# An adaLN block with cached attention on one core: K and V loaded in pairs of tiles, all of K ahead of all of V

## The chip, the cores and the metric

The kernel runs on one NeuronCore of a Trainium2 chip. The core has a matrix engine (PE), a vector engine (DVE), a scalar engine (ACT), a general engine (POOL), a sequencer that here only issues transfers (SP), and 16 DMA engines that move bytes between the device memory (HBM) and the core's own memory. The metric is the device time of one execution in microseconds. Every transfer counts: inputs start in HBM and the output ends there.

## The reference

A transformer block for two sequences (B = 2), one new token each, model width D = 640, 32 heads of 192. Of the key and value caches only the last W = 1024 of 4096 positions are read. Cut to what matters:

```python
W = min(4096, max(256, Sk // 4))                       # 1024
q = (x @ wq).reshape(B, 1, 32, 192).transpose(0, 2, 1, 3)
k, v = k_cache[:, :, Sk - W:, :], v_cache[:, :, Sk - W:, :]
p = softmax(einsum('bhqd,bhkd->bhqk', q, k) * 192 ** -0.5)
a = einsum('bhqk,bhkd->bhqd', p, v).reshape(B, 1, 6144) @ wo

sa, ca, ga, sb, cb, gb = (silu(c) @ w_mod).reshape(B, 6, 1, 640)   # one each
h = layernorm(x) * (1 + ca) + sa
x = x + ga * attention(h)                              # the four lines above
h = layernorm(x) * (1 + cb) + sb
x = x + gb * ((gelu(h @ w_gate) * (h @ w_up)) @ w_down)
```

Everything is bf16 in HBM: `w_mod` 4.9 MB, `wq` and `wo` 7.9 MB each, the K and V parts 25.2 MB each, the three FFN weights 2.0 MB each. Each byte is read once.

## The kernel before, in words

**The layout of the attention.** The 128 partitions hold 32 heads times 4 groups of positions, so each partition owns 256 consecutive positions of one head for each sequence. A tile is 64 of them for all partitions: 64 * 192 values, 24576 bytes in a row, 3.1 MB in all. One sequence (b) has four K tiles and four V tiles (t = 0 to 3).

**Scores** (`d_mul` L452, `p_reduce` L458, `d_rows` L472). For each half tile (hf) DVE multiplies K in place by the query, which `qbc` holds on every partition (L454). PE then adds up the products: 12 matmuls of 512 columns with the identity as the weights (L465), 16 of the 192 products at a time into one PSUM bank, and DVE sums the 16 that are left into 32 scores (L474). `filler` puts four matmuls that nobody reads (L444) ahead of each such group.

**Softmax** (`softmax` L478), once for each sequence: DVE, PE and ACT pass a maximum along, ACT takes the exponentials (L493).

**Values** (`d_mask` L501, `p_pv` L506). DVE spreads the 64 weights of each partition into `Em`, a matrix with one column for each head and position (L502, two buffers), and PE multiplies it with the V tile: 32 matmuls of 384 columns for each tile (L514). `normalize` (L523) and `p_sel` (L536) bring the result into the layout of `wo`.

**What sets the order.** A recording layer (`_Sched`) keeps one list of operations for each engine, in the order in which the code declares them, and derives each wait from the buffers that an operation reads and writes. `emit` (L83) writes the five lists out, inside an `nc.Block()` (L665) that gives each engine its own block of code, entered and left by a branch. All large loads are issued by SP, in the order of its list.

**The ring.** K and V go through five slots of one tile each (`ring`, NS = 5). The order is the four K tiles of b = 0; then V of b = 0 and K of b = 1 in turn; then V of b = 1 (`items`, L322). A slot is loaded again as soon as the last reader of its tile has been declared and has finished (`declare_ring` L332). Ahead of the ring come `w_mod` (into slots 2 and 3) and `wq` in two parts (into `r1`, 61440 bytes a partition); behind it `wo` in four parts (into `r1` again, L585), `w_gate`, `w_up` in two parts and `w_down` in three (into slots that are free by then, L589 to L601).

**The work beside it.** While K of b = 1 is scored, V of b = 0 is multiplied (the loop at L546); V of b = 1 comes alone (L562). Then `oc` and its transposes `oT` (L578), the `wo` product in four parts (L609), layer norm, the FFN (L628, L651) and the store of 2.5 KB. `warm` (L440) puts matmuls without a reader between these small stages too, for instance 14 behind the second `p_sel`, 15 behind the second part of `wo`, 13 beside the second layer norm, 7 behind the first part of `w_down`.

Of the kernel before, what the change touches and what calls it, by code (L numbers as in the profile page):

```python
# [103 lines left out]
def bass_adaLN_cond__sliding_block_cached__geglu_ffn__decode_kernel(  # L104
# [34 lines left out]
    NTL = KP // J  # L139
    JH = J // 2  # L140
    NQ = H * Dh
# [4 lines left out]
    NQC = RN // QC  # L146
    SCALE = float(Dh) ** -0.5
# [6 lines left out]
    NS = 5  # L154
    SL = J * Dh
    WQ_SPLIT = [3, 2]
    assert sum(WQ_SPLIT) == KT
    WO_SPLIT = [16, 16, 12, 4]
    OT_SPLIT = [16, 16, 16]
    assert sum(WO_SPLIT) == NT and sum(OT_SPLIT) == NT  # L160
    WU_SPLIT = [3, 2]
    assert sum(WU_SPLIT) == KT
    WD_SPLIT = [6, 4, 2]
    assert sum(WD_SPLIT) == FT
    ND = 4

    WO_WARM = [2, 15, 2, 10]
    WD_WARM = [7, 2, 0]

    es = ExitStack()  # L170
    with es:
# [6 lines left out]
        ring = sb("ring", [P, NS, J, Dh], BF16)  # L178
        ring_f = ring[:, :, :, :].rearrange("p s j d -> p (s j d)")
        def slot_f(slot, a, n):  # L180
            assert a + n <= SL
            return ring_f[:, slot * SL + a:slot * SL + a + n]


        assert KT * 6 * D <= 2 * SL and 2 * KT * F + FT * D <= 2 * SL
        wm_f = ring_f[:, 2 * SL:2 * SL + KT * 6 * D]
        wm_v = wm_f.rearrange("p (k n) -> p k n", k=KT)
        Qsel = slot_f(4, 0, 2 * HM * P).rearrange("p (b m n) -> p b m n", b=2, m=HM)
        qC = slot_f(4, 2 * HM * P, RN)
        wg_v = ring_f[:, SL:SL + KT * F].rearrange("p (k n) -> p k n", k=KT)  # L190
        wu_v = ring_f[:, SL + KT * F:SL + 2 * KT * F].rearrange("p (k n) -> p k n", k=KT)
        wd_v = ring_f[:, SL + 2 * KT * F:SL + 2 * KT * F + FT * D].rearrange("p (f n) -> p f n", f=FT)
        oc = slot_f(4, 0, RN)
        oT = slot_f(4, RN, NT * SQ).rearrange("p (t m) -> p t m", m=SQ)
        aC = slot_f(3, 0, FN)
        aT = slot_f(3, FN, FT * SQ).rearrange("p (f m) -> p f m", m=SQ)
# [3 lines left out]
        one = sb("one", [1, 1], F32)  # L200
# [20 lines left out]
        Sg = sb("Sg", [P, max(KP, FN)], F32)  # L221
        S_sb = Sg[:, 0:KP]
        gl = Sg[:, 0:FN]
        ones_f = Sg[:, 0:P]
        M1 = sb("M1", [P, 1], F32)
        gm = sb("gm", [1, H], F32)
        gx = sb("gx", [1, H, QP], F32)
        nb = sb("nb", [P, 1], F32)
        E_sb = sb("E_sb", [P, KP], BF16)
# [7 lines left out]
        BK_O = 3  # L237
# [13 lines left out]
        sem_wq = [S.sem("d_wq%d" % i) for i in range(len(WQ_SPLIT))]  # L251
        sem_wo = [S.sem("d_wo%d" % i) for i in range(len(WO_SPLIT))]
        sem_wg = S.sem("d_wg")
        sem_wu = [S.sem("d_wu%d" % i) for i in range(len(WU_SPLIT))]
        sem_wd = [S.sem("d_wd%d" % i) for i in range(len(WD_SPLIT))]
        sem_ring = [S.sem("d_ring%d" % i) for i in range(NS)]
# [9 lines left out]
        def dram_rows(v):  # L266
# [7 lines left out]
        S.op("pool", lambda e: e.memset(one[:, :], 1.0), writes=["one"], name="one")  # L274
        S.op("pool", lambda e: e.memset(ones_f, 1.0), writes=[("S", 0, 0), ("S", 0, 1), ("S", 1, 0), ("S", 1, 1)], name="ones_f")
        S.op("pool", lambda e: e.affine_select(out=ident_f[:, :], in_=ones_f, pattern=[[-1, P]],
                                                compare_op=ALU.is_equal, fill=0.0, base=0, channel_multiplier=1),
             reads=[("S", 0, 0), ("S", 0, 1), ("S", 1, 0), ("S", 1, 1)], writes=["ident_f"], name="ident_f")
# [3 lines left out]
        S.op("pool", lambda e: e.memset(Qsel, 0.0), writes=[("ring", 4, 0)], name="Qsel0")  # L282
# [18 lines left out]
        for b in range(2):  # L301
            for m in range(HM):
                S.op("dve", (lambda b, m: lambda e: e.tensor_copy(
                    out=Qsel[:, b, m, :].rearrange("p (a m t) -> p a m t", a=NJ, m=HM)[:, :, m, :],
                    in_=ident_f[:, BS * b:P:SQ].unsqueeze(2).broadcast_to([P, NJ, QP])))(b, m),
                    reads=["ident_f"], writes=[("ring", 4, 0)], name="Qsel%d%d" % (b, m))

        def half_key(slot, hf):
            return ("ring", slot, hf)

        def ring_keys(slot):
            return [half_key(slot, 0), half_key(slot, 1)]

        keep = {}
        S.dma("sp", k_dma(wm_f, w_mod.rearrange("(p k) n -> p (k n)", k=KT)), sem_wm, writes=ring_keys(2) + ring_keys(3), name="ld_wm")
        wq_src = A_wq.rearrange("(p k) n -> p k n", k=KT)
        wq_of = [(sum(WQ_SPLIT[:i]), sum(WQ_SPLIT[:i + 1])) for i in range(len(WQ_SPLIT))]
        keep["wq_dma"] = [S.dma("sp", k_dma(wq_v[:, ka:kb, :].rearrange("p k n -> p (k n)"), wq_src[:, ka:kb, :].rearrange("p k n -> p (k n)")),
                                sem_wq[i], writes=[("wq", i)], name="ld_wq%d" % i) for i, (ka, kb) in enumerate(wq_of)]


        items = [("k", 0, t) for t in range(NTL)]  # L322
        for t in range(NTL):
            items += [("v", 0, t), ("k", 1, t)]
        items += [("v", 1, t) for t in range(NTL)]
        place = {it: n for n, it in enumerate(items)}
        ring_state = {"next": 0, "done": set()}

        def slot_of(*it):
            return place[it] % NS  # L330

        def declare_ring(*consumed, upto=len(items)):  # L332
            ring_state["done"].update(place[it] for it in consumed)
            while ring_state["next"] < upto and (ring_state["next"] < NS or (ring_state["next"] - NS) in ring_state["done"]):
                n = ring_state["next"]
                kind, b, t = items[n]
                slot = n % NS
                cache = A_v_cache if kind == "v" else A_k_cache
                S.dma("sp", k_dma(ring[:, slot, :, :].rearrange("p j d -> p (j d)"),
                                  cache[b, :, K0:Sk, :].rearrange("h (q r) d -> h q r d", q=QP)[:, :, J * t:J * (t + 1), :].rearrange("h q r d -> h q (r d)")),  # L340
                      sem_ring[slot], writes=ring_keys(slot), name="ld_%s%d_%d" % (kind, b, t))
                ring_state["next"] += 1

        declare_ring(upto=2)


# [37 lines left out]
        def mod_part(part):  # L384
# [10 lines left out]
            S.op("pe", f, reads=["scT"] + ring_keys(2) + ring_keys(3), writes=[bank(bk)], name="mod%d" % part)  # L395
# [9 lines left out]
        declare_ring(upto=4)  # L405


        for i, (ka, kb) in enumerate(wq_of):
            def f(e, ka=ka, kb=kb):
                last = None  # L410
                for k in range(ka, kb):
                    for c in range(NQC):
                        for j in range(NJ):
                            last = e.matmul(ps[SQ * j:SQ * j + SQ, BK_H + c, 0:QC], lhsT=hT[:, k, :],  # L414
                                            rhs=wq_v[:, k, RN * j + QC * c:RN * j + QC * (c + 1)],
                                            start=(k == 0), stop=(k == KT - 1), tile_position=(0, SQ * j), skip_group_check=True)
                return last
            keep["q"] = S.op("pe", f, reads=["hT", ("wq", i)], writes=[bank(BK_H + c) for c in range(NQC)], name="q%d" % i)

# [5 lines left out]

        for c in range(NQC):
            move(("act", "dve")[c % 2], qC[:, QC * c:QC * (c + 1)], ps[:, BK_H + c, 0:QC], [bank(BK_H + c)], [("qC", c)], "qC%d" % c)

        def f(e):
            last = None  # L430
            for b in range(2):
                for m in range(HM):
                    last = e.matmul(ps[:, BK_O, b * Dh:(b + 1) * Dh], lhsT=Qsel[:, b, m, :], rhs=qC[:, m * Dh:(m + 1) * Dh],  # L433
                                    start=(m == 0), stop=(m == HM - 1), skip_group_check=True)
            return last
        S.op("pe", f, reads=[("qC", c) for c in range(NQC)] + ring_keys(4), writes=[bank(BK_O)], name="qsel")
        move("act", qbc[:, :, :].rearrange("p b d -> p (b d)"), ps[:, BK_O, 0:2 * Dh], [bank(BK_O)], ["qbc"], "qbc")
        declare_ring()

        def warm(n, bk):  # L440
            def f(e):
                last = None
                for _ in range(n):
                    last = e.matmul(ps[:, bk, 0:2 * Dh], lhsT=ident_b[:, :], rhs=qbc[:, :, :].rearrange("p b d -> p (b d)"),  # L444
                                    start=True, stop=True)
                return last
            S.op("pe", f, reads=["ident_b", "qbc"], writes=[bank(bk)], name="warm")

        def filler(n=1):
            warm(n * ND, BK_W)  # L450

        def d_mul(b, t, hf):  # L452
            ks = slot_of("k", b, t)
            S.op("dve", lambda e: e.tensor_tensor(out=ring[:, ks, hf * JH:(hf + 1) * JH, :], in0=ring[:, ks, hf * JH:(hf + 1) * JH, :],  # L454
                                                  in1=qbc[:, b, :].unsqueeze(1).broadcast_to([P, JH, Dh]), op=ALU.mult),
                 reads=["qbc"], writes=[half_key(ks, hf)], name="mul%d_%d_%d" % (b, t, hf))

        def p_reduce(b, t, hf):  # L458
# [10 lines left out]
            if hf == 1:  # L469
                declare_ring(("k", b, t))  # L470
# [245 lines left out]
```

## Time and profile before

| | |
|---|---|
| three runs | 189.08, 189.10, 189.87 us; median 189.1 us |
| profiled execution: first to last instruction (its span) | 187.5 us |
| what lies around the span, by the median | 1.6 us |
| bytes read from HBM | 76.88 MB, 410 GB/s over the span |
| busy: PE, DVE, ACT, POOL | 131.9, 107.1, 13.9, 4.9 us |
| busy: the DMA queue that SP fills, share of 16 engines | 96.3% |
| transfers: SP, ACT | 30, 2 |

Times in the profile count from the start of the span. A group in the profile has the line of the code, the engine, the tile written and the tiles read, the shapes, then `busy, mean ns of one`, and behind the second bar the time for which the engine sat idle ahead of it and what ended most of that. Matmuls and the weight loads that go with them (PEld) are recorded apart. "PEclk" is the clock granted to the matrix engine, 9 or 1.0 for full and 5 or 0.50 for half. For DMA the trace has each packet (one row of one partition, with its size and the time it took) and, for each transfer, the moment at which each of the 16 DMA engines had finished its share; a reader of the tile waits for the last of the 16.

### The profile page before, as it was taken

Reading aid. Unit: us, or ns where it says so; the run is one execution under the profiler, and the core shown is the slowest. Engines: PE = TensorE matmul, PEld = TensorE weight load, DVE = VectorE, ACT = ScalarE, POOL = GpSimd, SP = SyncE. Lnnn points to the kernel's source line nnn. Section 1 sums busy time; section 2 is a strip of 40 time slices with the busy share of each in tenths; the row PEclk is TensorE's granted clock in tenths of the full one; section 3 lists DMA queues with packets and bytes.
Section 4 is the critical chain, followed back from the end, with each engine's and each line's share of the span. In section 5 each row is a group of like instructions: output and inputs, shape, how many; then the busy total and the mean of one; then the engine's idle time right before and its main releaser. Section 6 shows DMA issues by size and latency. Waiting matters only on the chain.

```text
span 187.5 us, 2388 instructions
## 1 busy us (share of the span) xinstructions
PE 131.9 (70%) x1068; PEld 65.3 (35%) x1068; DVE 107.1 (57%) x114; ACT 13.9 (7%) x24; POOL 4.9 (3%) x12
## 2 busy tenths in 40 slices
PE   0004543565999989449999939929539998859993
PEld 0001221251443333125454514504225656535441
DVE  6811400029599998389599398298475602903431
ACT  2003200031000000000000000000010002300400
POOL 8100000000000000000000000000000000000000
PEclk9999999555699999966999996987957999999999
DMA  7999899999999999999999999999999999999980
GB/s 262 394 457 440 385 454 412 425 451 440 435 425 421 419 418 440 451 430 430 425 419 412 430 456 435 428 419 425 419 435 446 427 424 424 421 412 420 414 345 5
DMA packets 4221, 77.02 MB, mean 411 GB/s; under 512 B 500, under 2 KB 500, under 8 KB 1140
## 3 DMA queue, kind: packets, MB, share of 16 engines
q1 hardware_dynamic: 4188, 76.88, 96.3%
q8 instruction: 8, 0.13, 0.3%
q10 hardware_dynamic: 24, 0.01, 0.0%
q14 instruction: 1, 0.01, 0.0%
HBM read 76.88 MB, written 0.00 MB: 410 GB/s over the span
## 4 chain that ended last, share of the span: by engine, by line
DMA 53%; PE 21%; DVE 20%; issue 2%; SPq 2%; ACT 0%; DVEq 0%
DMA ring<-in_A_k_cache_dram 31%; DMA r<-in_A_wo_dram 22%; DVE ring L454 14%; PE ps L465 8%; PE ps L444 5%; PE ps L514 4%; DVE Sg L474 2%; SPq L260 2%; PE ps L609 1%; DVE Em L502 1%; PE ps L628 1%; PE ps L651 1%; DVE ring L348 0%; ACT E_sb L493 0%; DVE ring L642 0%
## 5 line engine op out<-in xcount | busy, mean ns | idle before, releaser
L454 DVE TENSOR_TENSOR ring<-ring,qbc 128x6144 bf16<-128x6144 bf16 x16 | 53.5, 3352 | 10.6 <-DMA ring<-in_A_k_cache_dram 10.6
L465 PE MATMUL ps<-ring,ident_b 128*128 128x512 bf16 x192 | 50.0, 416 | 10.9 <-DVE ring L454 10.8
L444 PE MATMUL ps<-qbc,ident_b 128*128 128x384 bf16 x174 | 34.6, 333 | 2.9 <-issue 2.2
L465 PEld LDWEIGHTS ps<-ring,ident_b 128*128 128x128 bf16 x192 | 19.2, 104 | 38.5 <-DVE ring L454 15.0
L514 PE MATMUL ps<-ring,Em 128*64 128x384 bf16 x256 | 26.3, 367 | 4.9 <-DVE Em L502 4.9
L444 PEld LDWEIGHTS ps<-qbc,ident_b 128*128 128x128 bf16 x174 | 15.9, 100 | 18.5 <-issue 8.4
L514 PEld LDWEIGHTS ps<-ring,Em 128*64 128x64 bf16 x256 | 15.4, 122 | 15.0 <-DVE Em L502 6.4
L502 DVE TENSOR_TENSOR Em<-E_sb,M32b 128x2048 bf16<-128x2048 bf16 x8 | 18.2, 2283 | 4.0 <-PE ps L514 4.0
L474 DVE TENSOR_REDUCE Sg<-ps 128x32 f32<-128x512 f32 x16 | 11.0, 687 | 9.1 <-PE ps L465 9.1
L391 PE MATMUL ps<-ring,scT 128*32 128x480 bf16 x40 | 4.4, 601 | 14.9 <-DMA ring<-in_w_mod_dram 14.9
L414 PE MATMUL ps<-r,hT 128*32 128x384 bf16 x80 | 6.8, 523 | 8.8 <-DMA r<-in_A_wq_dram 8.8
L424 DVE CAST ring<-ps 128x384 bf16<-128x384 f32 x4 | 2.0, 553 | 15.7 <-PE ps L414 14.7
L414 PEld LDWEIGHTS ps<-r,hT 128*32 128x32 bf16 x80 | 3.1, 140 | 12.7 <-issue 6.0
L391 PEld LDWEIGHTS ps<-ring,scT 128*32 128x32 bf16 x40 | 1.3, 133 | 16.3 <-issue 16.3
L528 ACT ACTIVATE On<-ps,rden 32x192 bf16<-32x192 f32 x4 | 1.6, 412 | 71.1 <-PE ps L514 61.3
L532 DVE TENSOR_SCALAR On<-ps,rden 32x192 bf16<-32x192 f32 x4 | 1.7, 418 | 7.4 <-ACT On L528 7.4
L616 DVE TENSOR_TENSOR lnt<-ps,modC 128x160 f32<-128x160 f32 x1 | 0.3, 324 | 7.3 <-PE ps L609 7.3
L609 PE MATMUL ps<-r,ring 128*32 128x160 bf16 x192 | 4.1, 233 | 0.5 <-DVE ring L578 0.5
L578 DVE STREAM_TRANSPOSE ring<-ring 128x512 bf16<-128x512 bf16 x3 | 4.1, 1423 | 0.1
L493 ACT ACTIVATE E_sb<-Sg,nb 128x256 bf16<-128x256 f32 x2 | 1.0, 507 | 40.8 <-DVE nb L492 40.8
L609 PEld LDWEIGHTS ps<-r,ring 128*32 128x32 bf16 x192 | 3.3, 96 | 1.9 <-issue 1.5
L433 PE MATMUL ps<-ring 128*128 128x192 bf16 x16 | 2.7, 361 | 1.2 <-DVE ring L424 1.2
(68 smaller groups left out, 54.7 us busy)
## 6 DMA issues: line engine op xcount, KB each, us to landing
ring<-in_A_k_cache_dram SPq DMA_DIRECT2D x8, 3072.0 KB, 29.6
ring<-in_A_v_cache_dram SPq DMA_DIRECT2D x8, 3072.0 KB, 25.1
r<-in_A_wo_dram SPq DMA_DIRECT2D x2, 2560.0 KB, 37.9
ring<-in_w_mod_dram SPq DMA_DIRECT2D x1, 4800.0 KB, 14.0
r<-in_A_wq_dram SPq DMA_DIRECT2D x1, 4608.0 KB, 24.5
r<-in_A_wq_dram SPq DMA_DIRECT2D x1, 3072.0 KB, 32.6
r<-in_A_wo_dram SPq DMA_DIRECT2D x1, 1920.0 KB, 44.5
ring<-in_B_w_gate_dram SPq DMA_DIRECT2D x1, 1920.0 KB, 18.0
```

The costliest lines, as they stand in the source:

```text
L260: return lambda e: e.dma_start(dst, src)
L391: last = e.matmul(ps[SQ * j:SQ * j + SQ, bk, 0:3 * DN].rearrange("p (i n) -> p i n", i=3), lhsT=scT[:, k, :], rhs=wm_v[:, k, 3 * part * D: ...
L414: last = e.matmul(ps[SQ * j:SQ * j + SQ, BK_H + c, 0:QC], lhsT=hT[:, k, :], rhs=wq_v[:, k, RN * j + QC * c:RN * j + QC * (c + 1)], start=( ...
L433: last = e.matmul(ps[:, BK_O, b * Dh:(b + 1) * Dh], lhsT=Qsel[:, b, m, :], rhs=qC[:, m * Dh:(m + 1) * Dh], start=(m == 0), stop=(m == HM - ...
L444: last = e.matmul(ps[:, bk, 0:2 * Dh], lhsT=ident_b[:, :], rhs=qbc[:, :, :].rearrange("p b d -> p (b d)"), start=True, stop=True)
L454: S.op("dve", lambda e: e.tensor_tensor(out=ring[:, ks, hf * JH:(hf + 1) * JH, :], in0=ring[:, ks, hf * JH:(hf + 1) * JH, :], in1=qbc[:, b ...
L465: last = e.matmul(o_ap, lhsT=ident_b[:, :], rhs=ring[:, ks, hf * JH:(hf + 1) * JH, ci * GC:(ci + 1) * GC], start=(ci == 0), stop=(ci == NC ...
L474: S.op("dve", lambda e: e.tensor_reduce(out=S_sb[:, a:a + JH], in_=ps[:, hf, 0:JH * GC].rearrange("p (j c) -> p j c", j=JH), axis=AX.X, op ...
L502: S.op("dve", lambda e: e.tensor_tensor(out=Em[:, t % 2, :, :], in0=E_sb[:, J * t:J * (t + 1)].unsqueeze(2).broadcast_to([P, J, H]), in1=M ...
L514: last = e.matmul(ps[r:r + 2 * H, BK_O, 0:ON], lhsT=Em[:, t % 2, 2 * jp:2 * jp + 2, :].rearrange("p j c -> p (j c)"), rhs=ring[:, vs, 2 * ...
L578: S.op("dve", (lambda t0, nt: lambda e: e.transpose(oT[:, t0:t0 + nt, :], oc.rearrange("p (q k) -> p k q", k=NT)[:, t0:t0 + nt, :]))(t0, n ...
L609: last = e.matmul(ps[SQ * j:SQ * j + SQ, BK_M, 0:DN], lhsT=oT[:, t, :], rhs=wo_v[:, t, DN * j:DN * j + DN], start=(t == 0), stop=(t == NT ...
```

## The change

Two tiles become a pair of 128 positions: rows of 49152 bytes, 6.3 MB, eight transfers for K and V instead of sixteen. The order is all of K (b = 0, then b = 1), one softmax for both sequences, then all of V. The ring gives way to three places, two in `pp` and one in `r1`, where `wq` was; the eight pairs go to places 0, 1, 2, 0, 1, 2, 0, 1. `wo` then goes over place 2, the FFN weights over place 0. `wq` and `w_up` come in one transfer each, `wo` and `w_down` in two, so SP issues 17 transfers instead of 30. `oc`, `oT`, `Qsel` and a few more get memory of their own.

Of the matmuls with the identity only the first of a group still loads the weights; the others (`held`) are issued without a weight load. The four matmuls without a reader ahead of each score group stay; all others are gone, those of the V phase and of the stages behind it. The query product uses 512 columns instead of 384. `nc.Block()` is gone: each list is emitted straight. Behind the first sequence's `normalize`, ACT issues seven loads of k rows by 8k bytes (k = 1, 2, 4, 6, 8, 10, 12) from `wq` into a tile `mk` that nothing reads; SP waits for them at the end.

```diff
+    NP = 3
+    SL = PJ * Dh
+    WO_SPLIT = [32, 16]
...
-    WU_SPLIT = [3, 2]
-    assert sum(WU_SPLIT) == KT
-    WD_SPLIT = [6, 4, 2]
+    WD_SPLIT = [10, 2]
     assert sum(WD_SPLIT) == FT
-    ND = 4
-
-    WO_WARM = [2, 15, 2, 10]
-    WD_WARM = [7, 2, 0]
+    NF = 4
+    MARKS = [1, 2, 4, 6, 8, 10, 12]
...
+        pp = sb("pp", [P, 2, PJ, Dh], BF16)
+        pp_f = pp[:, :, :, :].rearrange("p s j d -> p (s j d)")
+        assert SL <= KT * NQ and KT * 6 * D <= SL and 2 * KT * F + FT * D <= SL
...
+        S.dma("sp", k_dma(wq_v.rearrange("p k n -> p (k n)"), A_wq.rearrange("(p k) n -> p (k n)", k=KT)),
+              sem_wq, writes=place_keys(2) + ["wq"], name="ld_wq")
+
+        items = [(kind, b, t) for kind in ("k", "v") for b in range(2) for t in range(NPR)]
+        place_of = {it: k for it, k in zip(items, (0, 1, 2, 0, 1, 2, 0, 1))}
+        state = {"next": 0}
+
+        def load_next():
+            it = items[state["next"]]
+            state["next"] += 1
+            kind, b, t = it
+            k = place_of[it]
+            cache = A_v_cache if kind == "v" else A_k_cache
+            S.dma("sp", k_dma(places[k].rearrange("p j d -> p (j d)"),
+                              cache[b, :, K0:Sk, :].rearrange("h (q r) d -> h q r d", q=QP)[:, :, PJ * t:PJ * (t + 1), :].rearrange("h q r d -> h q (r d)")),
+                  sem_pl[k], writes=place_keys(k), name="ld_%s%d_%d" % (kind, b, t))
+
+        load_next()
...
+        S.op("pe", f, reads=["hT", "wq"] + place_keys(2), writes=[bank(BK_H + c) for c in range(NQW)], name="q")
+        load_next()
...
+        def held(e, out, lhsT, rhs, start, stop):
+            i = mybir.InstMatmult(name=nc.get_next_instruction_name(), engine=mybir.EngineType.PE,
+                                  ins=[e.lower_ap(rhs), e.lower_ap(lhsT)], outs=[e.lower_ap(out)],
+                                  start_tensor_calc=start, stop_tensor_calc=stop, tile_size=(P, P), tile_position=(0, 0), ldweights=False)
+            return e.add_instruction(i)
 
         def warm(n, bk):
             def f(e):
                 last = None
-                for _ in range(n):
-                    last = e.matmul(ps[:, bk, 0:2 * Dh], lhsT=ident_b[:, :], rhs=qbc[:, :, :].rearrange("p b d -> p (b d)"),
-                                    start=True, stop=True)
+                for i in range(n):
+                    put = e.matmul if i == 0 else lambda *a, **k: held(e, *a, **k)
+                    last = put(ps[:, bk, 0:2 * Dh], lhsT=ident_b[:, :], rhs=qbc[:, :, :].rearrange("p b d -> p (b d)"),
+                               start=True, stop=True)
                 return last
...
+        def softmax():
+            sk = [[("S", b, t, q) for t in range(NPR) for q in range(NH)] for b in range(2)]
             S.op("dve", lambda e: e.tensor_reduce(out=M1[:, :], in_=S_sb, axis=AX.X, op=ALU.max),
-                 reads=sk, writes=["M1"], name="pmax%d" % b)
...
+            for b in range(2):
+                S.op("act", (lambda b: lambda e: e.activation(out=E_sb[:, b, :], in_=S_sb[:, b, :], func=ACTF.Exp, scale=SCALE, bias=nb[:, b:b + 1],
+                                                              accum_out=esum[:, b:b + 1]))(b),
+                     reads=sk[b] + ["nb"], writes=[("E", b), ("esum", b)], name="exp%d" % b)
+            S.op("pe", lambda e: e.matmul(ps[:, BK_T, P + 2:P + 4], lhsT=DS[:, :], rhs=esum[:, :], start=True, stop=True),
+                 reads=[("esum", 0), ("esum", 1), "DS"], writes=[bank(BK_T)], name="den")
...
+            k = place_of["v", b, t // 2]
...
-        steps = [(b, t, hf) for b in range(2) for t in range(NTL) for hf in range(2)]
-        for n, (b, t, hf) in enumerate(steps):
-            if b == 1 and hf == 0:
-                if t == 0:
-                    d_rows(*steps[n - 1])
-                    softmax(0)
-                d_mask(0, t)
-            d_mul(b, t, hf)
-            if b == 1 and hf == 0:
-                p_pv(0, t)
-            filler()
-            p_reduce(b, t, hf)
-            if n > 0 and not (b == 1 and t == 0 and hf == 0):
+        steps = [(b, t, q) for b in range(2) for t in range(NPR) for q in range(NH)]
+        for n, (b, t, q) in enumerate(steps):
+            d_mul(b, t, q)
+            warm(NF, BK_W)
+            p_reduce(b, t, q)
+            if n > 0:
                 d_rows(*steps[n - 1])
-        normalize(0)
+            if q == NH - 1 and state["next"] < 6:
+                load_next()
         d_rows(*steps[-1])
-        softmax(1)
-        for t in range(NTL):
-            d_mask(1, t)
-            p_pv(1, t)
-            if t < NTL - 1:
-                filler(2)
-            else:
-                p_sel(0)
-        normalize(1)
-        warm(4, 1)
+        softmax()
+        d_mask(0, 0)
+        d_rden()
+        for b in range(2):
+            for t in range(NTL):
+                if b or t:
+                    d_mask(b, t)
+                p_pv(b, t)
+                if t % 2 == 1 and state["next"] < len(items):
+                    load_next()
+                if b == 1 and t == 2:
+                    p_sel(0)
+            normalize(b)
+            if b == 0:
+                for i, k in enumerate(MARKS):
+                    S.dma("act", k_dma(mk[0:k, 64 * i:64 * i + 4 * k], A_wq[0:k, 64 * i:64 * i + 4 * k]), sem_mk, name="mark%d" % k)
+        assert state["next"] == len(items)
         p_sel(1)
-        warm(14, 1)
...
-                  sem_wo[i], writes=[("wo", i)], deps=keep["wq_dma"] + [keep["q"]], name="ld_wo%d" % i)
-        assert slot_of("k", 1, NTL - 1) == 1 and slot_of("v", 1, 0) == 2
-        r3_dead = [keep["red", 1, NTL - 1], keep["pv"]]
+                  sem_wo[i], writes=[("wo", i)], deps=[keep["pv", 0, NTL - 1]], name="ld_wo%d" % i)
+        assert place_of["v", 0, NPR - 1] == 2 and place_of["v", 1, 0] == 0
+        dead = [keep["pv", 1, NTL // 2 - 1]]
         S.dma("sp", k_dma(wg_v.rearrange("p k n -> p (k n)"), B_w_gate.rearrange("(p k) n -> p (k n)", k=KT)), sem_wg,
-              writes=["wg"], deps=r3_dead, name="ld_wg")
...
+              writes=["wg"], deps=dead, name="ld_wg")
+        S.dma("sp", k_dma(wu_v.rearrange("p k n -> p (k n)"), B_w_up.rearrange("(p k) n -> p (k n)", k=KT)), sem_wu,
+              writes=["wu"], deps=dead, name="ld_wu")
...
-            if WO_WARM[i]:
-                warm(WO_WARM[i], 1)
...
-        warm(13, 1)
...
-        with nc.Block() as block:
-            def sp_tail(e):
-                e.wait_ge(sem_out, 16)
-
...
+        S.emit("sp", nc.sync)
+        nc.sync.wait_ge(sem_out, 16)
+        nc.sync.wait_ge(sem_mk, 16 * len(MARKS))
+        S.emit("act", nc.scalar)
+        S.emit("pool", nc.gpsimd)
+        S.emit("dve", nc.vector)
+        S.emit("pe", nc.tensor)
```

## The prediction, before the run

> **What bounds the kernel now.** I read the 40 slices first, then the DMA queues, then the chain that ended last, then the timeline of its end.
>
> ```profile
> PEclk9999999555699999966999996987957999999999
> DMA  7999899999999999999999999999999999999980
> GB/s 262 394 457 440 385 454 412 425 451 440 435 425 421 419 418 440 451 430 430 425 419 412 430 456 435 428 419 425 419 435 446 427 424 424 421 412 420 414 345 5
> ...
> q1 hardware_dynamic: 4188, 76.88, 96.3%
> q8 instruction: 8, 0.13, 0.3%
> ```
>
> The DMA engines are busy in every slice but the first and the last; no compute engine is. 96.3% of 187.5 us is 180.6 us, and from the first packet (1.8) to the last landing of a weight (183.6) there are 181.8. So the stream never stands still, whatever DVE and PE do beside it: time comes off only where the packets get shorter, or ahead of and behind the stream. In the trace a packet of 24576 bytes takes 914 ns (median), one of 36864 takes 1364, one of 38400 takes 1420: about 36.8 ns for each 1000 bytes and 9 to 10 ns for the packet itself. One engine carries 8 rows of each tile, and K and V tiles land 7.31 us apart: 8 * 914. Nothing is lost between two transfers.
>
> The chain of waits, in order of time, for the score steps, the wait for `wo` and the end:
>
> ```profile
> 51.16 3.27 DVE ring L454
> 54.43 0.60 DVE Sg L474
> ...
> 82.81 5.35 PE ps L514 x32
> ...
> 123.12 40.39 DMA r<-in_A_wo_dram
> 163.50 0.04 issue
> 163.55 1.29 PE ps L609 x64
> ...
> 181.68 0.60 PE ps L651 x24
> 182.27 1.24 PE ps L444 x7
> 183.52 0.39 PE ps L651 x16
> 183.91 0.43 PE ps L444 x2
> 184.34 0.28 PE ps L651 x8
> ```
>
> A score step is 3.27 + 0.60 = 3.87 us of DVE. At the end, the last 320 KB of `w_down` land at 183.58 by the landing records, but PE reaches them at 184.34: nine matmuls without a reader (L444, 1.24 + 0.43) stand in its line. The timeline has the same group at both clocks and the output's way out:
>
> ```profile
> 139.64 4.24 PE L514 MATMUL ps<-ring,Em 128*64 128x384 bf16 x32 [2.45 <-DVE Em L502]
> ...
> 153.47 2.79 PE L514 MATMUL ps<-ring,Em 128*64 128x384 bf16 x32
> ...
> 185.36 0.69 SPq L260 DMA_DIRECT2D out_dram<-sc  x1
> ```
>
> PV takes 5.35 us at half clock, 4.24 where the clock rises inside it, 2.79 at full.
>
> **Part 1: longer rows, fewer transfers.** By the slope above a row of 49152 bytes takes 1364 + 12288 * 0.0368 = 1816 ns against 2 * 914: 12 ns less, 64 rows on each engine, 0.77 us. `wq` (914 + 1364 to 2268): 10 ns * 8. `wo` (765 + 765 + 578 + 196 to 1514 + 765): 25 ns * 8. `w_up` 9 * 8, `w_down` 6 * 8. Together **1.1 us**; the bytes are the same. Bounds: 0 (a long row is cut up and pays as before) and 1.2. The last V pair then lands at 151.46 - 0.85 = 150.6, the last of `wo` at 168.6, `w_up` at 177.8, the last of `w_down` at 182.5.
>
> **Part 2: does the stream stay full?** All of K first makes DVE the slower one: a pair needs 4 * 3.87 = 15.5 us, and comes every 8 * 1.816 = 14.5. K starts at 48.8 (pair landed) instead of 41.7. The query is ready: `q` in one piece waits for `wq` to 34.2, then 60 matmuls of 512 columns, four side by side, at half clock about 6.6 us (L391: 480 columns, 20 matmuls, 2.19 us), then 4.5 us as now: 45.3. Before, DVE lost 2.0 us in the first steps to a cold PE (50.47 instead of 48.4); I keep that. The last product is done at 48.8 + 2.0 + 16 * 3.87 - 0.6 = 112.1, its PE group at 115. The third V pair waits for that, and the first DMA engine runs dry at 119.4: 4 us to spare. The other pairs have 9 or more. The fourth V pair waits for PV of tile 1: softmax to 118.6 (0.7 rows, 0.7 maximum, 2.2 from maximum to exponent as at 77.8 to 80), mask 2.3, PV cold 5.35, PV 2.8 to 5.4, so 129 to 132 against 134. `wo` waits for 135 to 138 against 148. So **0 us**, with 2 to 5 us of cover.
>
> **Part 3: the end.** PV of the last two tiles now both follow 150.6; PE has stood still for some 9 us, so its clock is low. PV 4.8 (between 4.24 and 5.35), `p_sel` 0.83, PV 2.79: 159.0, where it is 156.2 now. `normalize` 2.0, `p_sel` and `oc` 2.0, two transposes 2.8 (as now from 156.2 to 163): `wo` starts at 165.8. Its 192 matmuls are 3 * 1.29 at full clock, about 6.6 at half; without the fillers the clock is low at first, so I take 5.6: 171.4 (171.5 now). Layer norm 4.5 as now: 175.9. `w_gate` 1.0 to 1.8, `w_up` from 177.8 on, 1.8: 179.6. GeGLU and its transpose 1.6: 181.2. The ten blocks of `w_down` land at 181.7, take 0.9 to 1.6, then two blocks 0.3: the last matmul ends at **183.3** instead of 184.62, 1.3 us earlier. Bounds: 182.85 (right behind the landing) and 184.5 (half clock throughout: PV +0.55, `wo` +1.0, the rest less 0.35 of slack).
>
> **Part 4: the block.** Its exit shows in SP's waits as 0.2 us, its entry as 0.1 between the start barrier (0.7) and the first issue (0.80). I take 0.3; bounds 0 and 0.5.
>
> **Part 5: weight loads and marks.** PE issues 929 matmuls and 705 weight loads instead of 1068 of each, and the instruction stream takes DMA time too: eight packets of 16384 bytes, 1.02 to 1.11 us each, one for about 256 PE instructions. After the first (30.6) one engine lands 1.9 us behind the first, where the 16 had been within 0.57; at the end eight are, and the last is 2.0 behind. Six packets instead of eight still leave some engine 2 us late, and readers wait for the last one: 0, bounds -1.4 and 0. The Trainium skill ("Runtime: NRT & Kernel Launch", section "Instruction fetch mechanics") also has blocks of 16 KiB and 256 instructions, but calls the cost of one "mostly hidden"; the landings here disagree, and by the page the whole spread would be something else and this term 0 as well. The held matmuls are in no trace: with their loads twelve take 2.75 us (229 ns each), and the load runs beside the matmul, so I take 0 with bounds of 0 and +17% (below). The seven marks put at most seven packets and seven completions on one engine; 320 bytes took 19 ns and 4 bytes 9: 0 to 0.2 us, and I take 0.1 as inside the rounding. ACT issues them around 137 (0.55 us each) and needs nothing until 159.
>
> **Sum.** 187.5 - 1.3 - 0.3 = 185.9 in the span; the three runs' median stands 1.6 above the span: **187.5 us**.
>
> **Rivals.**
> *The cold end.* The fillers were there to hold the clock (0.98 to 1.0 in the last 36 us), and nothing holds it now. At half clock throughout the last matmul ends at 184.5: 187.5 + 1.2 = 188.7. For it: PE's share is small in every stage after 150. Against it: windows full of work get the full clock after 3 to 7 us (41.7 to 50.5). 14%.
> *The rows gain nothing*, the change in this part not doing what it says: landing at 183.6, last matmul 184.1, 188.3. Against it: the line through four sizes. 10%.
> *K stalls the stream (slower).* PE's group of 16 takes 0.81 + 2.75 = 3.56 us beside DVE's 3.87. If held matmuls are slower, because each drains before the next, PE sets the step; from 3.87 + 4.2 / 15 = 4.15 us on (17% over the present group) the third V pair is late and the stream stands still. At 4.4 us: 15 * 0.53 - 4.2 = 3.8 us, so 191.3. For it: no row shows one. Against it: less work per matmul. 16%.
> *Each transfer has a fixed cost.* The 2.5 KB store takes 1.7 us from issue to landing; were that paid in line, 13 fewer transfers would save 22: 165. Against it: tiles land 8 * 914 ns apart. 2%. The Trainium skill ("DMA: Bandwidth & Descriptors", "Anatomy of one DMA") fits 2.0 us a transfer, 26 us here, but calls most of it completion latency, which a full queue hides, as the landings show.
>
> **How the numbers follow.** The forecast has 58%; within it the bounds of parts 1, 3 and 4 give 186.6 to 188.3. A measurement of this kernel tells about 0.5%, 0.95 us, from no change: 188.15 to 190.05. Faster: nearly all of the forecast, the fixed cost and the edges of the first two rivals, 62%. Same: the rest of those, 22%. Slower: the stall, 16%. The range reaches from 186.6 to 189.4 and leaves out the stall and the fixed cost.
>
> **What would show it.** Packets of 49152 bytes at 1816 ns; `w_down` landing at 182.5; K steps of 3.87 us and DVE idle only ahead of the first pair; no gap in the DMA slices at 115 to 135; the first PV behind 150.6 at 4.2 to 5.4 us; the last matmul close behind the last landing. A DMA slice below 9 in the middle, or a score step above 4.15 us, would prove me wrong; so would a last matmul at 184.5.

## The result, and the profile after

| | before | after |
|---|---|---|
| first comparison: median (range) of 12 times each | 189.8 (188.98 to 190.34) | 188.38 (186.9 to 189.16) |
| the same kernel again (29 and 12 times) | 189.1 (188.77 to 190.48) | 188.36 (186.92 to 188.98) |
| ratio after / before, 95% interval | | 0.9942 [0.9921, 0.9962]; again 0.9945 [0.9923, 0.9968] |
| traced execution: its time; its span | 189.08; 187.5 | 187.32; 186.1 |

So the change makes the kernel about 0.6% faster, 1.1 us. The forecast was 1.6 us and 187.5 us. The sign held, and so did what was said of the transfers; the gain was forecast too large by about a half, because the end of the kernel does not go as described. (The median of before was 189.1 to 189.8 in the comparisons of this study, its shortest execution 188.77 to 188.98. The experiments below come from three sessions on different chips, so differences of medians from two sessions are good to 0.2 or 0.3 us.) One execution, the traced one of `b_both` below, took 377 us, with the 512-column matmuls of PE at 1094 ns on average instead of 416 while DVE's product took its usual 3350, and is left out.

The slices and queues of the changed kernel's page:

```profile
PEclk9999999997557999999999999858975969966758
DMA  7999999898999989898999999998989999899980
...
q1 hardware_dynamic: 2316, 76.88, 96.5%
q8 instruction: 6, 0.10, 0.2%
q10 hardware_dynamic: 110, 0.01, 0.0%
```

The stream is as full as before (8 or 9 in every slice but the ends), with 2316 packets instead of 4188, and six packets of code instead of eight, as worked out. The clock of PE (first line) is the new thing: in the last nine slices (from 145 us on), where before it stood at 9, it goes up and down between 5 and 9. The chain of waits, first the score steps, then the end:

```profile
58.34 3.27 DVE pp L437
61.61 0.60 DVE Sg L457
...
129.03 21.95 DMA pp<-in_A_v_cache_dram
150.98 0.14 issue
151.12 4.13 PE ps L503 x32
155.25 0.77 PE ps L528 x8
156.01 2.74 PE ps L503 x32
...
165.53 6.08 PE ps L592 x144
171.61 0.87 issue
172.48 0.26 PE ps L592 x2
...
177.54 3.42 PE ps L608 x36
...
182.55 1.04 PE ps L626 x48
```

Up to 165.5 nearly every piece lies where the forecast had it: score steps of 3.87, the last V pair at 151.0 (forecast 150.6), the last PV done at 158.8 (159.0), `wo` from 165.5 (165.8). Then `wo` takes until 172.7 where 171.4 was forecast, and inside it stands a line that no semaphore explains: 0.87 us of "issue" with two of 192 matmuls left. In before the same kind of line had been in the chain, 2.21 us in the middle of a row of 15 fillers:

```profile
164.84 1.24 PE ps L444 x7
166.08 2.21 issue
168.30 1.48 PE ps L444 x8
```

I had read over it.

### The profile page after: what moved, and what is told of

It reads as the page before. It is cut to its first block, busy times and chain, and to the rows that moved or that the text cites. A ratio compares the mean times of both kernels' runs of the same rounds, so it can differ in the third digit from the quotient of the medians.

```text
span 186.1 us, 1860 instructions
## 1 busy us (share of the span) xinstructions
PE 111.8 (60%) x933; PEld 36.6 (20%) x709; DVE 105.6 (57%) x108; ACT 14.0 (8%) x24; POOL 4.8 (3%) x11
## 3 DMA queue, kind: packets, MB, share of 16 engines
q1 hardware_dynamic: 2316, 76.88, 96.5%
## 4 chain that ended last, share of the span: by engine, by line
DVE 39%; DMA 37%; PE 20%; issue 1%; ACT 1%; SPq 0%; DVEq 0%
DMA pp<-in_A_k_cache_dram 25%; DVE pp L437 19%; DMA pp<-in_A_v_cache_dram 12%; PE ps L503 8%; DVE r L437 7%; DVE Sg L457 5%; PE ps L423 4%; PE ps L592 3%; PE ps L608 2%; DVE oT L565 2%; DVE Em L488 1%; PE ps L528 1%; PE ps L626 1%; DVE oc L404 1%; PE ps L450 1%
## 5 line engine op out<-in xcount | busy, mean ns | idle before, releaser
L437 DVE TENSOR_TENSOR pp<-pp,qbc 128x6144 bf16<-128x6144 bf16 x12 | 40.1, 3348 | 9.3 <-DMA pp<-in_A_k_cache_dram 9.3
L423 PE MATMUL ps<-pp,ident_b 128*128 128x512 bf16 x132 | 32.8, 400 | 0.0
L503 PE MATMUL ps<-pp,Em 128*64 128x384 bf16 x192 | 23.1, 416 | 10.4 <-DVE Em L488 5.7
L503 PEld LDWEIGHTS ps<-pp,Em 128*64 128x64 bf16 x192 | 13.8, 141 | 19.2 <-DVE Em L488 6.2
L437 DVE TENSOR_TENSOR r<-r,qbc 128x6144 bf16<-128x6144 bf16 x4 | 13.4, 3345 | 0.0
L450 PE MATMUL ps<-pp,ident_b 128*128 128x512 bf16 x12 | 4.9, 406 | 13.3 <-DVE pp L437 13.3
L423 PE MATMUL ps<-qbc,ident_b 128*128 128x384 bf16 x48 | 10.7, 333 | 0.0
L423 PE MATMUL ps<-r,ident_b 128*128 128x512 bf16 x44 | 10.2, 379 | 0.0
L592 PE MATMUL ps<-r,oT 128*32 128x160 bf16 x192 | 6.3, 322 | 5.0 <-DVE oT L565 4.1
L430 PEld LDWEIGHTS ps<-qbc,ident_b 128*128 128x128 bf16 x16 | 1.6, 101 | 37.8 <-issue 37.8
L592 PEld LDWEIGHTS ps<-r,oT 128*32 128x32 bf16 x192 | 6.0, 140 | 5.4 <-issue 5.4
L430 PE MATMUL ps<-qbc,ident_b 128*128 128x384 bf16 x16 | 5.4, 338 | 0.7 <-ACT qbc L402 0.7
```

Source lines behind the costliest of these rows:

```text
L423: return e.add_instruction(i)
L430: last = put(ps[:, bk, 0:2 * Dh], lhsT=ident_b[:, :], rhs=qbc[:, :, :].rearrange("p b d -> p (b d)"), start=True, stop=True)
L437: S.op("dve", lambda e: e.tensor_tensor(out=places[k][:, JH * q:JH * (q + 1), :], in0=places[k][:, JH * q:JH * (q + 1), :], in1=qbc[:, b, ...
L450: last = put(o_ap, lhsT=ident_b[:, :], rhs=places[k][:, JH * q:JH * (q + 1), ci * GC:(ci + 1) * GC], start=(ci == 0), stop=(ci == NCH - 1))
L503: last = e.matmul(ps[r:r + 2 * H, BK_O[b], 0:ON], lhsT=Em[:, t % 2, 2 * jp:2 * jp + 2, :].rearrange("p j c -> p (j c)"), rhs=places[k][:, ...
L592: last = e.matmul(ps[SQ * j:SQ * j + SQ, BK_M, 0:DN], lhsT=oT[:, t, :], rhs=wo_v[:, t, DN * j:DN * j + DN], start=(t == 0), stop=(t == NT ...
```

## The experiments

Three theories were set against each other. A: PE at half clock behind the last V pair is what eats the gain and makes the times of the changed kernel spread over 2 us. B: the stream's last landing moves between executions. C: PE waits for its own code, in the line just shown.

**The changed kernel again, and without the seven loads.**

```diff
-                for i, k in enumerate(MARKS):
-                    S.dma("act", k_dma(mk[0:k, ...
-        nc.sync.wait_ge(sem_mk, 16 * len(MARKS))
```

> The changed kernel once more, unaltered, for a second trace and a narrower ratio. The first 12 times went from 186.9 to 189.16 us, and the one traced execution (187.32) is among the short ones. Theory A (the end at half clock): executions differ in how long the products behind the last V pair take, so this trace, if its span is longer than 186.1, has its last landing of w_down still at 183.1 and the last matmul later than 183.6. Theory B (the stream): the last landing itself moves between executions, one DMA engine falling behind by more than 2 us, and the last matmul follows it. Ratio by both about 0.994.

> The changed kernel without the seven small loads and without SP's wait for them. Theory A and the prediction's part 5: 0.1 us shorter at most, so no difference that can be told. Rival (the marks disturb the stream while V runs, the first-landing spacing of the V pairs grew from 14.53 to 14.67 us beside them): 0.2 to 0.5 us shorter.

Measured: 188.36 us [0.9923, 0.9968] and 188.32 us [0.9915, 0.9973]. The marks cost nothing that can be told. Both traced executions are longer than the first (spans 186.8 and 188.1), yet their last landings are earlier: 182.69 and 182.70 against 183.12. B falls. What is longer lies behind the last V pair: the first product with V there takes 4.9 and 5.3 us instead of 4.1, `w_down` takes 1.79 in both instead of 1.01, and the product with `wo` ends at 172.9 and 174.2 instead of 172.7. The matmuls of `wo`, and of `w_down` for the first, from the timelines of the two:

```profile
165.94 4.82 PE L592 MATMUL ps<-r,oT 128*32 128x160 bf16 x190 [4.10 <-DVE oT L565]
172.68 0.24 PE L592 MATMUL ps<-r,oT 128*32 128x160 bf16 x2 [1.92 <-issue]
...
182.54 1.79 PE L626 MATMUL ps<-pp,aT 128*32 128x160 bf16 x48 [1.61 <-DVE aT L329]
```

```profile
166.48 5.21 PE L589 MATMUL ps<-r,oT 128*32 128x160 bf16 x190 [4.10 <-DVE oT L562]
173.94 0.25 PE L589 MATMUL ps<-r,oT 128*32 128x160 bf16 x2 [2.25 <-issue]
```

The pause comes behind the 190th matmul each time, whatever the clock did before (0.71 granted in the first, 0.65 in the second): it belongs to a place in the code. Where the first 190 matmuls went faster (4.82 and 5.21 us instead of 6.08) the pause was longer (1.92 and 2.25 instead of 0.87), so the clock alone does not set the end of the product. A packet of 16384 bytes on the instruction queue starts at 170.4 and 171.4, and PE goes on 2.3 and 2.5 us later; in the first trace at 170.1, 2.4 us ahead of the end of the pause.

**Fewer instructions far ahead of the end.** `a_shift` leaves 35 PE instructions out, `a_ldw` adds 224, `a_ctrl` adds 48, all of them in the score steps:

```diff
 # a_shift
-            warm(NF, BK_W)
+            if n < 9:
+                warm(NF, BK_W)
 # a_ldw: in warm and in p_reduce; a_ctrl: in warm alone
-                    put = e.matmul if i == 0 else lambda *a, **k: held(e, *a, **k)
+                    put = e.matmul
```

> The changed kernel with the fillers of the last 7 of 16 score steps left out: 35 PE instructions fewer, all of them 50 us and more ahead of the end. In three traces PE stood still for 0.87, 1.92 and 2.25 us with 2 of the 192 wo matmuls left, and went on 2.3 to 2.5 us after a packet of 16384 bytes on the instruction queue had started. Theory C (code comes late): the border between two blocks of 256 PE instructions lies 4 instructions ahead of the end of the wo product, where PE takes them fastest; 35 fewer put it into the layer norm, where PE waits anyway. So no such pause in wo, the last matmul 0.9 to 2 us earlier but no earlier than 183.0, the median at 187.2 to 187.6 and the spread smaller. Theory A alone (half clock): the pause has another cause, the median stays at 188.3.

> The changed kernel with a weight load ahead of every matmul with the identity, as before the change: 224 PE instructions more in the score steps, nothing altered behind them. Theory C: 224 more move the block borders of the wo product by 256 - 224 = 32 the same way as a_shift does, the pause leaves the last matmuls of wo, and the kernel with more instructions is faster, 187.2 to 187.7. Theory A alone, and the prediction's part 5 (weight loads run beside the matmuls): 188.3, no difference. Held matmuls being worth something: slower than 188.3, DVE's score step above 3.87 us.

> The changed kernel with the weight loads back in the 16 groups of four fillers alone: 48 PE instructions more, none behind the scores. A control for a_shift: here too PE's stream is shifted, but the block border stays inside the wo product, 52 instead of 4 instructions ahead of its end. Theory C: the pause stays, now with 26 matmuls left, and the time stays at 188.0 to 188.6. Rival (any shift helps, or the fillers that a_shift left out were what cost): 187.6.

Measured: `a_shift` 187.60 (187.52 to 187.85), ratio 0.9889 [0.986, 0.9919]; `a_ldw` 187.57 (187.45 to 187.92), 0.989 [0.9862, 0.9917]; `a_ctrl` 188.08 (187.56 to 189.41), 0.9933 [0.991, 0.9955]. The timelines of the three, in that order:

```profile
165.36 6.20 PE L593 MATMUL ps<-r,oT 128*32 128x160 bf16 x192 [4.10 <-DVE oT L566]
...
182.15 1.79 PE L627 MATMUL ps<-pp,aT 128*32 128x160 bf16 x48 [2.42 <-DMA pp<-in_B_w_down_dram]
```

```profile
165.59 6.30 PE L592 MATMUL ps<-r,oT 128*32 128x160 bf16 x192 [4.10 <-DVE oT L565]
```

```profile
167.26 4.73 PE L592 MATMUL ps<-r,oT 128*32 128x160 bf16 x166 [4.10 <-DVE oT L565]
173.50 0.71 PE L592 MATMUL ps<-r,oT 128*32 128x160 bf16 x26 [1.52 <-issue]
```

C holds to the instruction. Two edits that go opposite ways, 35 fewer and 224 more, move the border by nearly the same amount modulo 256 (35 and 32 instructions), out of `wo` and into `w_gate` (the layer norm, as forecast for `a_shift`, is too short to hold it), and both take the pause and the spread away; 48 more leave it in, with the 26 matmuls that were forecast. Counted over PE's records (matmuls and weight loads), the pause comes behind exactly 1459 instructions in all eight traces of changed kernels that have it, whatever was put in or left out ahead of it, and behind 1710 in before and `b_noblock`; with the semaphore instructions that the trace has of PE's queue these are 1473 and 1729, 256 apart. A border alone does not stop PE: the changed kernel, `a_shift`, `a_ldw` and `a_ctrl` all have another one 256 instructions from the first, in the first half of `wo`, and no pause there.

A kernel that issues 224 instructions more is 0.8 us faster than one without them. The pause costs about 0.75 us in the median (188.36 to 187.60; by the two ratios 1.1). It does not cost that in each execution: the shortest of the changed kernel (186.92) are shorter than any of `a_shift` (187.52). They have no trace, so the reason is open; the first trace shows one way, `w_down` at full clock. A weight load ahead of a matmul costs nothing in the score steps: DVE's product is 3346 ns in `a_ldw`, 3348 in the changed kernel, and the steps wait for DVE in both.

**Fillers back at the end.**

```diff
+                if b == 1 and t == 1:
+                    warm(24, 2)
...
+        warm(8, 2)
         p_sel(1)
+        warm(16, 2)
...
+            warm((6, 10)[i], 1)
...
+        warm(13, 1)
...
+        warm(4, 1)
         ffn_gu(BK_G[1], wu_v, "wu", "wu", 0, KT)
+        warm(8, 1)
```

> The changed kernel with matmuls without a reader put back behind the scores: 24 behind the second V tile of b = 1, 8 and 16 around the second p_sel, 6 and 10 behind the parts of wo, 13 beside the second layer norm, 4 and 8 around w_up, most of them without a weight load. Theory A: PE runs the end at full clock, PV behind the last landing takes 2.8 us instead of 4.1, the 192 matmuls of wo about 4 instead of 7, the last matmul sits right behind the last landing in every execution, and the median falls by about 1 us to 187.2 to 187.5. Theory B: the median stays within 0.3 us of the changed kernel's, because the last landing sets the end.

Measured: 186.75 us (186.61 to 186.87), ratio 0.9866 [0.9842, 0.989], shorter than either theory had it. The clock in four stretches (V, `wo`, FFN, `w_down`) of the changed kernel and of this one; the columns are the stretch, its length, the busy time of PE, PEld, DVE, ACT and POOL, then the granted clock, DMA share and GB/s:

```profile
151.00:155.30 4.30, 4.18 (x34) 2.78 (x35) 0.00 (x0) 0.00 (x0) 0.00 (x0) 0.67 1.05 452
165.50:171.60 6.10, 6.07 (x190) 5.91 (x191) 1.22 (x1) 0.00 (x0) 0.00 (x0) 0.55 1.00 425
177.50:181.00 3.50, 3.39 (x40) 1.40 (x40) 0.00 (x0) 0.49 (x1) 0.00 (x0) 0.50 0.91 376
182.50:183.60 1.10, 1.01 (x48) 0.81 (x48) 0.00 (x0) 0.00 (x0) 0.00 (x0) 1.00 0.01 5
```

```profile
150.50:153.30 2.80, 2.75 (x33) 2.16 (x34) 0.00 (x0) 0.00 (x0) 0.00 (x0) 1.00 1.05 454
163.60:170.70 7.10, 4.97 (x199) 3.47 (x194) 1.21 (x1) 0.00 (x0) 0.00 (x0) 1.00 0.99 421
175.30:179.10 3.80, 2.73 (x45) 1.03 (x42) 0.01 (x1) 0.49 (x1) 0.00 (x0) 1.00 1.00 422
182.00:183.10 1.10, 1.01 (x48) 0.83 (x48) 0.01 (x1) 0.00 (x0) 0.00 (x0) 1.00 0.01 5
```

In the changed kernel PE runs at 0.50 to 0.67 in the first three stretches (and at 1.00 in `w_down` in this trace, the short one), with the fillers at 1.00 in all four. The slack that this makes also takes in the code: of `wo`, from the timeline of `a_fill`,

```profile
168.71 0.80 PE L596 MATMUL ps<-r,oT 128*32 128x160 bf16 x33 [1.60 <-DMA r<-in_A_wo_dram]
170.00 0.73 PE L596 MATMUL ps<-r,oT 128*32 128x160 bf16 x31 [0.50 <-issue]
...
182.03 1.01 PE L634 MATMUL ps<-pp,aT 128*32 128x160 bf16 x48 [1.51 <-DMA pp<-in_B_w_down_dram]
```

PE waits for the transfers again, the pause is still there (0.50) and costs nothing, and the last matmul (183.04) sits 0.4 us behind the last landing (182.67). Against `a_shift`, which has no pause but a cold end, that is 0.85 us more in the median (from two sessions; the ratios give 0.4), and in the traces the last matmul ends at 183.04 instead of 183.94 with the last landing at the same place (182.67 and 182.64). Against the changed kernel in the same session it is 1.6 us. So A holds as well: the half clock has a price of its own, beside the pause.

**The rows.** Each pair in two transfers, readers waiting for both; on the changed kernel and on `a_fill`:

```diff
-            S.dma("sp", k_dma(places[k]...
+            for h in range(2):
+                S.dma("sp", k_dma(places[k][:, J * h:J * (h + 1), :]...
```

> The changed kernel with each pair loaded in two transfers of 24576-byte rows, readers still waiting for both. The prediction's part 1: 64 packets more on each engine, 12 ns each, so the last V pair and the last landing 0.8 us later (183.5 to 183.9) and the time 0.6 to 0.8 us longer, 189.0. Rival (long rows gain nothing, or their gain is lost in the end): the same landing as the changed kernel, 182.7 to 183.1, and 188.3.

> a_fill (fillers back at the end) with each pair in two transfers of 24576-byte rows, readers waiting for both. a_fill went from 186.61 to 186.87 us, so a small price shows here. The prediction's part 1: last landing 0.7 to 0.8 us later than in a_fill (182.67), and since the end follows the landing there, 187.4 to 187.6. Rival (row length is worth nothing, the 0.5 us of a_rows were spread): 186.75.

Measured: 188.87 (188.06 to 189.86), ratio 0.9962 [0.9938, 0.9986]; and 187.34 (187.15 to 187.68), 0.9886 [0.9862, 0.991]. On the first the spread hides most of it; on the second 0.6 us stand clear of both ranges, and the last landing is at 183.53 against 182.67. So the long rows are worth what part 1 of the prediction gave them for K and V (0.77 us at the landing; here 0.86, and 0.6 in the time).

**The kernel before, without the block, without the fillers, without both.**

```diff
-        with nc.Block() as block:
+        S.emit("sp", nc.sync)
...
-                filler(2)
```

> The kernel before with the five lists emitted straight, without nc.Block(); nothing else altered. The prediction's part 4: 0.3 us shorter (0 to 0.5) in the span. The traced executions also differ in what lies around the span (1.6 us before, 1.2 after), so if that belongs to the block as well, 0.6 to 0.8 us shorter in the time. Rival: straight lists fetch their code differently at the start and nothing is gained.

> The kernel before without the matmuls without a reader behind the scores (those ahead of each score group stay). Theory A: PE falls to half clock behind the last V tile, the last matmul is no longer held up by the 1.67 us of fillers in its line but by slow products and by code that comes late, and the time is about the same to 0.7 us longer, with a wider spread than before (188.8 to 190.5). The prediction's reading of before (fillers stand in the way of the last group by 0.7 to 1.1 us): 188.3 to 188.6.

> The kernel before without the block and without the fillers behind the scores, that is without the pairs, the new order, the fewer transfers and the held matmuls. The two parts alone gave 188.2 and 188.8 against 189.1 to 189.4. If they add up: 187.8 to 188.1, so that these two edits alone are worth as much as the whole change. Rival: the change's order and rows carry the gain, and this stays at 188.2 or above.

Measured: without the block 188.22 (187.95 to 189.19), ratio 0.9962 [0.9942, 0.9982]; without the fillers 188.76 (188.6 to 188.91), 0.9944 [0.9919, 0.997]; without both 187.89 (187.86 to 188.14, five executions), 0.992 [0.9896, 0.9944]. The block's price has two halves. From the last matmul to the end of the span it is 2.49 us without it and 2.87 with it. And what lies around the span is 1.74 us in the median with the block (1.75 in `b_nofill`) and 1.21 to 1.37 in every execution without it. Without the fillers the product with `wo` has no pause, and each of its parts starts when its transfer lands:

```profile
163.59 2.32 PE L605 MATMUL ps<-r,ring 128*32 128x160 bf16 x64 [2.49 <-DMA r<-in_A_wo_dram]
168.19 2.32 PE L605 MATMUL ps<-r,ring 128*32 128x160 bf16 x64 [2.28 <-DMA r<-in_A_wo_dram]
```

So in before the fillers at the end cost time, although without them PE runs at half clock (0.50 granted) from 161 us to the end: they stand in PE's line, and they are code, which ran out in the middle of them. Which of the two carries the gain was not tried apart. The times also draw together, to 0.3 us where before spreads over 2.8 in the same session. Theory A alone had both wrong (it forecast no gain to a loss, and a wider spread); the prediction's reading of before was right in sign and near in size. Dropping the block and the fillers alone is worth 0.8%, no less than the whole change.

**The fastest version that the runs pointed to.** `a_fill` without the marks and with the fillers of the last 7 score steps left out, as in `a_shift`.

> a_fill without the seven small loads and without the fillers of the last 7 score steps: the fastest version that the runs point to. The end follows the last landing, and fewer instruction blocks and no marks can move that by 0.1 us at most: 186.6 to 186.8, the same as a_fill.

Measured: 187.16 us, three executions at 186.73 to 186.82 and three at 187.49 to 187.83; 0.9882 [0.9854, 0.991]. A miss: the 35 instructions fewer moved the border in the second part of `wo` from 31 to 13 matmuls ahead of its end, and the pause in the traced execution, one of the short ones, is 0.79 us instead of 0.50. Whether it is longer still in the three long ones is open, since they have no trace. `a_fill` stays the fastest, 1.3% below before.

## Why the prediction came out as it did

**Part 1, the rows: right in kind, a little large.** A packet of 49152 bytes takes 1815 ns (forecast 1816). The last landing is 0.5 us earlier in the first trace and 0.9 in the next ones (182.6 to 182.7; forecast 182.5, 1.1 earlier).

**Part 2, the stream stays full: right.** The score steps take 3.87 us. The third V pair is issued at 114.8 (forecast 115) with the first engine dry at 119.8; the rival *K stalls the stream* never came near. Nothing in it hung on the held matmuls, which are worth nothing by themselves.

**Part 3, the end: this is where it failed.** The step read: "Its 192 matmuls are 3 * 1.29 at full clock, about 6.6 at half; [...] I take 5.6: 171.4". Measured from the first to the last of them: 7.2, 7.0 and 7.7 us in the three traces, end at 172.7, 172.9 and 174.2. The matmuls themselves took 6.1, 4.8 and 5.2 us, near what was put down for them; the pause for code, 0.87 to 2.25 us, is what was missing. Without it the product takes 6.2 to 6.3 (`a_shift`, `a_ldw`) and the time is 187.6. That this is the forecast to 0.1 us is partly luck. In the trace of `a_shift` the last matmul ends at 183.94 and not at 183.3: the first ten blocks of `w_down` land at 182.0 instead of 181.7, and all twelve take 1.79 at half clock, as in six of the seven traces of the changed kernel and its kin without fillers, where the sum had 1.6 in the middle of its bounds. What part 4 gave too little (below) makes up for most of that.

**Part 5, the code: the step behind that failure.** It weighed the packets of code only as traffic on the DMA engines and put them at 0. They count as something that PE waits for. The trace of before showed it, as a pause of 2.21 us without a releaser, 0.3 us behind the start of such a packet, and I asked neither of that line what PE was waiting for nor of the new kernel where its borders would lie. The place in before (behind 1710 instructions, 256 to a block) and the new kernel's 933 matmuls and 709 weight loads put a border into the last four matmuls of `wo`. (The prediction's 929 and 705 are each four short of what the trace has.) The Trainium skill ("Runtime: NRT & Kernel Launch", section "Instruction fetch mechanics") says that crossing a 16 KiB border is "mostly hidden". In the score steps it is: 18 instructions in 3.87 us. In `wo`, at 60 to 80 instructions in a microsecond, it is not.

**Part 4, the block: right in the span, short around it.** 0.4 us in the span (forecast 0.3), and 0.5 around it, which the sum had carried over unaltered. (It carried over 1.6, from the one traced execution; the median of before is 1.74.) This made up for part of part 3.

**The rivals.** *The cold end* (188.7, 14%) comes nearest to what happened, with a second cause beside the one that it named. The price of the clock by itself is 0.85 us, against the 1.2 of that rival, by `a_fill` and `a_shift`. PE stands still for 4.1 us ahead of `wo` and starts it at half clock. The Trainium skill's page "TensorE: Matmul & The Clock Gate" (Part 1) gives half rate after an idle window of some 3.4 us; the traces agree in that the granted clock changes at steps of 3.41 us, but the window ahead of the drop at 164.1 was not idle throughout, PE was busy for a fifth of it. *The rows gain nothing* and *a fixed cost per transfer* are out by `a_fill_rows` and by the landings, 14.5 us apart for pairs.

The sum, in medians of the time: block -0.7 to -0.9, rows and transfers -0.6, fillers out of PE's line -0.7, which is what is left after the price of the lower clock; given back: 0.75 for code. That is -1.2 to -1.4, where the ratio gives -1.1. The parts were measured on different bases and need not add up; what the new order of K and V is worth by itself was not tried.

## What to carry to other kernels

Idle time of PE that nothing releases ("issue") beside a packet on the instruction queue was, here, PE waiting for its own code: look for it wherever many small matmuls run in a few microseconds, count the instructions ahead of them modulo 256, and move the border into a stage that waits anyway; that costs one line and was worth 0.4% here. The shift has to be tried, not only reckoned: in `a_fill_nm` it did not help. Fillers that hold the clock paid where PE would have waited anyway, and they are code too: the same idea cost time in before, and in the changed kernel it won 0.85 us beyond the pause. When the span is read from one trace, compare what lies around it as well; a change at the two ends of a program shows there.

## What the runs showed of the hardware that was not expected

- PE went on 2.3 to 2.6 us after the start of a packet of code, in all ten traces with the pause (in before 165.74 to 168.30), though the packet itself takes about 1 us. What fills the rest was not tried.
- The place of the pause follows from counting: 4 instructions ahead of the end of `wo` as built, 52 with 48 more. Both came out to the matmul.
- The `nc.Block()` cost 0.5 us outside the span, that no instruction in the span shows. Whether at its entry or its exit is open.
- In the first three traces of the changed kernel 19 to 44 of the 1024 packets of 49152 bytes took at least 60 ns longer than the median of 1815, most of them while K was multiplied; in `a_shift`, `a_ldw` and `a_ctrl` none did, and of those of 24576 bytes at most 7 of 2048. The cause is open.
